# First half of the gate and value weights: one tile by plain products, two tiles as one more Strassen set

## Chip, cores and metric

One core of one Trainium2 chip (trn2). The metric is the device time of one execution in microseconds, the median of several.

## What is computed

Three layers follow each other: a linear attention with a normalised output, a feed-forward layer with a rational activation, and a gated feed-forward layer. All inputs are float32.

```python
kv = np.einsum('bhsd,bhse->bhde', k, v)              # B=8, H=8, S=576, D=64
out = np.einsum('bhsd,bhde->bhse', q, kv)
rms = np.sqrt(np.mean(out * out, axis=-1, keepdims=True) + 1e-06)
x = (out / rms * g_norm)                             # -> 4608 x 512

h = x @ w_in                                         # 512 x 2048
g = (a0 + a1*h + a2*h*h + a3*h*h*h) / (1 + |b0|*|h| + |b1|*h*h + 1e-6)
x = g @ w_out                                        # 2048 x 512

g = x @ w_gate; val = x @ w_val                      # 512 x 1536 each
y = (g * sigmoid(g) * val) @ w_out2                  # 1536 x 512
```

## The kernel before

The 4608 tokens are nine tiles of N = 512. Every matrix operand is held as two fp32r parts, a high half (a copy on ACT) and a low half (the operand minus its high half, a `sub` on DVE or POOL), and every product is three matmuls, high by high, high by low, low by high (`mm3`, L107).

**First block** (L1129 to L1190). Each tile takes 16 steps f, one for 128 columns of `w_in`. A step has 12 matmuls of `h` for itself and 12 of `y` for the step two before (LAG = 2); ACT and DVE work out the activation in between, in `g_step` (L433) and `g_finish` (L419), and POOL makes the low half `ghl`. The attention of the next tile runs in the same steps. The weights of the block stay in the pool `w` (`w0` to `w31`); the outputs of a tile go to DRAM (`y_dram`, L74).

**Gate and value block.** The 1536 columns of each of the two weights are 12 units f of 128. Two ways are used. The *plain* one (`direct_mm`, L651) takes a tile and a unit with 24 matmuls: gate and value, four times 128 rows of the contraction, three matmuls each. The *Strassen* one (`gv_step`, L728) takes two tiles together (a set) and a unit with seven products of six matmuls, 42 for what takes 48 plainly. It needs seven combinations of the two tiles (`x_sum_ops`, L596, `x_combine`, L611) and seven of the unit's weights: four are halves of the weights themselves (`u_direct`, L508), three and their companions come from four sums (`u_sums`, L530; their halves in `u_late`, L545). The first six units (UP = 6) are the first half. In it tiles 0, 1 and 2 go plainly, unit by unit, three tiles each (L1348), and then the sets a, b and c (`seq`, L554); in the second half the sets are c, o (the two halves of tile 2), b, d (tiles 0 and 1), a.

**What sets the order.** The program is written in the order in which each engine shall run it; each engine runs its queue in that order, and SP issues all DMAs from one queue. Between the products of a step the table `fill` (filled by `put(set, unit, place, ...)`, L724) gives the places at which the preparations are issued: fetch of a unit's raw weights (`u_fetch`, L481, into two buffers each for gate and value), `u_scale` (two ACT and two DVE operations), `u_join` (two DVE operations), the halves, the sums; `x_fetch`, `x_sums`, `x_combine` for the next set (`prepare`, L1252). After the products of a plain unit `direct_post` (L663) multiplies on DVE and stores; the Strassen step leaves its sums to `post` (L697) in the following step. In the plain part before, the units of the second half were fetched, joined and put aside in DRAM too (`w_dram`, L479).

The two buffers that the prediction's steps touch are written here:

```python
663    def direct_post(f, n, ps):
664        g = late["work"].tile([P, N], F32, tag=("c", "d")[(3 * f + n) % 2], ...)
665        act(g, ps[0], AF.Silu)
666        tt(nc.vector, g, g, ps[1], ALU.mult)
667        g_store(n, f, g)
...
702            merge(i, 2, "c", ALU.subtract, "d")      # post(i, 0): writes the tile "d"
```

Of the kernel before, what the change touches and what calls it, by code (L numbers as in the profile page):

```python
# [15 lines left out]
P = 128  # L16
# [25 lines left out]
def fused_kernel(ctx: ExitStack, tc: tile.TileContext, kv_main, kv_left, q_t, w_in, w_out, w_gate, w_val, w_o2, ab, g_norm, out):  # L42
# [17 lines left out]
    x_p = ctx.enter_context(tc.tile_pool(name="x", bufs=1, side="left"))  # L60
    a_ctx = ExitStack()
# [18 lines left out]
    rows = w_p.tile([1, 3, P], F32, tag="w5", name="rows")  # L80
# [78 lines left out]
    wa_raw = ((at_p, "hl"), (s_p, "stg"), (at_p, "r0"), (w_p, "w6"), (w_p, "w7"))  # L159
# [332 lines left out]
    def u_join(f, compact=False):  # L492

        if not compact:
            run(join_ops(raw_u[f]), 2)
            val[f] = [w_views(r)[2] for r in raw_u.pop(f)]
            return
        c = late["p"].tile([P, 2, N], F32, tag="g", bufs=2, name="wc")
        for j, r in enumerate(raw_u.pop(f)):
            lo, hi, _ = w_views(r)  # L500
            stt(c[:, j, :].bitcast(I32), hi, 3, lo, ALU.logical_shift_left, ALU.bitwise_or)
        nc.sync.dma_start(out=w_dram[f], in_=c)
# [5 lines left out]
    def u_direct(f, eng):  # L508

        g, v = val[f]  # L510
        u = wu[f] = late[f"u{f % UP}"].tile([P, 2, 7, HK], F32R, tag=f"u{f % UP}", name="wu")
        u_halves(u, halves_of(g), slice(0, 7, 6), eng)
        u_halves(u, halves_of(v), slice(4, 6), eng)

    def u_first(eng):

        for src in val[0]:
            t = late["p"].tile([P, 2, 2, HK], F32R, tag="g", bufs=2, name="wu0")
            act(t[:, 0], halves_of(src))
# [3 lines left out]
    def u_again(eng):

        g, v = val[0]
        u = wu[0] = late["u0"].tile([P, 2, 7, HK], F32R, tag="u0", name="wu")
        u_halves(u, halves_of(g)[:, 1:2, :], slice(6, 7), eng)
        u_halves(u, halves_of(v), slice(4, 6), eng)

    def u_sums(f, tiles):  # L530
        g, v = val[f]
        m = sums[f] = tiles
        return [
            partial(tt, nc.vector, m[0][:, 0, :], g[:, :HK], g[:, HK:], ALU.add),
            partial(tt, nc.vector, m[0][:, 1, :], m[0][:, 0, :], v[:, :HK], ALU.subtract),
            partial(tt, nc.vector, m[1][:, 0, :], v[:, :HK], g[:, :HK], ALU.subtract),
            partial(tt, nc.vector, m[1][:, 1, :], v[:, HK:], m[0][:, 1, :], ALU.subtract),
        ]

    def u_early(f):  # L540
        tiles = [late["work"].tile([P, 2, HK], F32, tag=t, bufs=2, name="sm") for t in ("a", "b")]
        run(u_sums(f, tiles), 4)
        del val[f]

    def u_late(f, eng):  # L545
        for j, m in enumerate(sums.pop(f)):
            u_halves(wu[f], m, slice(2 * j, 2 * j + 2), eng)
# [81 lines left out]
    steps = [(q, f) for q in range(1, len(seq)) for f in range(UP if q > 3 else 0, NF2 if q > 3 else UP)]  # L629
# [334 lines left out]
    with tc.manual_schedule():  # L964
# [33 lines left out]
        po, pss, sqs, nb = {}, {}, {}, {}  # L998
# [410 lines left out]
```

## Time and profile before

| what | value |
|---|---|
| median of 3 runs | 1691.32 us (1690.96 to 1692.86) |
| profiled execution, its own time | 1692.0 us |
| its span, first to last instruction | 1689.9 us |
| mean granted TensorE clock | 0.999 |
| ACT busy in the span | 1061.2 us (63%) |
| POOL busy in the span | 540.8 us (32%) |
| first block ends, gate and value begins (PE) | at about 889.8 us |

The profile has, for each engine, the instructions with start, duration and what released an idle engine. "Busy" of PE is modelled, since matmuls overlap: a matmul of 512 columns is shown with 0.39 us though the next one starts earlier, so that pace is read from the starts. A line such as L92 is a helper (`act`), L95 is `sub`, L105 `stt`, L467 `tt`; the tile names tell which use it is: `gd` is the result of a plain unit, `e` and `gout` belong to a Strassen step, `sm` are weight sums, `wu` the weight halves, `wraw` the raw weights, `ysum` and `yraw` combinations of tiles, `xc` their halves. In the changed program the helper lines are 1 to 11 lines further down.

### The profile page before, as it was taken

To read this page: it belongs to the slowest core of one execution; us is meant where nothing else is said; L and a number is where in the kernel's file an instruction comes from. 1 tells how busy PE (TensorE), PEld (TensorE's weight loads), DVE (VectorE), ACT (ScalarE), POOL (GpSimd) and SP (SyncE) were. 2 spreads that over 40 slices of the span, in tenths; PEclk is the share of its full clock that TensorE was granted. 3 is DMA by queue.
4 is the path that set the end of the run, shared out by engine and by line. 5 is a ranking of instruction groups with operands and counts; after the bars stand their busy time and mean duration, and the time that the engine had idled before them with its cause. 6 is when DMAs were issued, how large, how long until landed. Compare 5 with 4: busy or idle time off the path is not lost. (4 is left out here: it accounts for less than half of the span.)

```text
span 1689.9 us, 24169 instructions
## 1 busy us (share of the span) xinstructions
PE 1673.4 (99%) x9088; PEld 1427.1 (84%) x9088; DVE 1335.7 (79%) x1824; ACT 1061.2 (63%) x1776; POOL 540.8 (32%) x376
## 2 busy tenths in 40 slices
PE   8999999999999999999999999999999999999999
PEld 5777888888888888888888888888888888999999
DVE  7999898899889898888886666666568858676665
ACT  7898787788787787877774444444435445444442
POOL 2113444434444443443331212212302156222221
PEclk9999999999999999999999999999999999999999
DMA  8861010010001010001117536132494354444431
GB/s 336 314 241 50 8 38 13 13 38 13 32 13 38 13 38 13 32 26 38 51 50 262 193 131 266 67 110 81 142 337 145 137 175 158 145 134 150 150 131 58
DMA packets 73529, 185.07 MB, mean 110 GB/s; under 512 B 6467, under 2 KB 35396, under 8 KB 71620
## 3 DMA queue, kind: packets, MB, share of 16 engines
q1 hardware_dynamic: 73412, 183.53, 31.0%
q8 instruction: 71, 1.16, 0.3%
q14 instruction: 46, 0.38, 0.1%
HBM read 121.64 MB, written 61.87 MB: 109 GB/s over the span
## 5 line engine op out<-in xcount | busy, mean ns | idle before, releaser
L95 POOL TENSOR_TENSOR ghl<-e,ghl 128x512 fp32r<-128x512 f32 x144 | 188.1, 1306 | 512.4 <-ACT ghl L92 218.8
L110 PE MATMUL pb<-xc,wu 128*128 128x512 f32 (+1 forms) x816 | 308.7, 378 | 0.0
L109 PE MATMUL pb<-xc,wu 128*128 128x512 f32 (+1 forms) x816 | 308.6, 378 | 0.0
L111 PE MATMUL pb<-xc,wu 128*128 128x512 f32 (+1 forms) x816 | 308.5, 378 | 0.0
L105 DVE SCALAR_TENSOR_TENSOR e<-e,e 128x512 f32<-128x512 f32 x288 | 229.0, 795 | 29.4 <-ACT e L92 23.1
L110 PE MATMUL y<-ghl,wt 128*128 128x512 f32 x576 | 226.1, 393 | 4.1 <-POOL ghl L95 4.0
L109 PE MATMUL y<-ghl,wt 128*128 128x512 f32 x576 | 227.1, 394 | 0.9 <-ACT ghl L92 0.9
L110 PE MATMUL ph<-x,wt 128*128 128x512 f32 x576 | 225.2, 391 | 1.2 <-POOL x L95 0.9
L109 PE MATMUL ph<-x,wt 128*128 128x512 f32 x576 | 225.7, 392 | 0.0
L111 PE MATMUL y<-ghl,wt 128*128 128x512 f32 x576 | 225.2, 391 | 0.0
L111 PE MATMUL ph<-x,wt 128*128 128x512 f32 x576 | 224.7, 390 | 0.0
L92 ACT ACTIVATE e<-pb 128x512 f32<-128x512 f32 (+1 forms) x144 | 82.2, 571 | 218.4 <-PE pb L111 218.4
L467 DVE TENSOR_TENSOR e<-e,pb 128x512 f32<-128x512 f32 (+1 forms) x192 | 124.5, 652 | 119.1 <-PE pb L111 72.1
L874 PE MATMUL pb<-wo,xo 128*128 128x256 f32 x756 | 214.1, 283 | 1.4 <-DVE sb L467 0.9
L875 PE MATMUL pb<-wo,xo 128*128 128x256 f32 x756 | 213.9, 283 | 0.0
L876 PE MATMUL pb<-wo,xo 128*128 128x256 f32 x756 | 213.9, 283 | 0.0
L109 PEld LDWEIGHTS pb<-xc,wu 128*128 128x128 f32 x816 | 153.3, 188 | 29.0
L110 PEld LDWEIGHTS pb<-xc,wu 128*128 128x128 f32 x816 | 153.3, 188 | 28.6
L111 PEld LDWEIGHTS pb<-xc,wu 128*128 128x128 f32 x816 | 153.3, 188 | 28.5
L92 ACT ACTIVATE xo<-graw 128x768 fp32r<-128x768 f32 x122 | 99.2, 840 | 114.6 <-DVE graw L467 52.0
L92 ACT ACTIVATE e<-ph 128x512 f32<-128x512 f32 x144 | 85.6, 594 | 112.0 <-PE ph L111 111.6
L874 PEld LDWEIGHTS pb<-wo,xo 128*128 128x128 f32 x756 | 145.1, 192 | 1.9 <-DVE sb L467 1.1
(140 smaller groups left out, 3428.7 us busy)
## 6 DMA issues: line engine op xcount, KB each, us to landing
graw<-gd SPq DMA_DIRECT2D x36, 768.0 KB, 4.6
gd<-gout SPq DMA_DIRECT2D x84, 256.0 KB, 2.2
kvm<-in_kv_main SPq DMA_DIRECT2D x32, 512.0 KB, 7.2
yraw<-yd SPq DMA_DIRECT2D x26, 512.0 KB, 6.0
q<-in_q_t SPq DMA_DIRECT2D x36, 256.0 KB, 2.7
yd<-sb SPq DMA_DIRECT2D x18, 512.0 KB, 3.3
out<-sb SPq DMA_DIRECT2D x17, 512.0 KB, 3.5
wraw<-in_w_in SPq DMA_DIRECT2D x16, 512.0 KB, 4.4
```

Source lines behind the costliest of these rows:

```text
L92: nc.scalar.activation(out=out, in_=in_, func=func, **kw)
L95: eng.tensor_tensor(out=out, in0=a, in1=b.bitcast(F32), op=ALU.subtract)
L105: nc.vector.scalar_tensor_tensor(out=out, in0=in0, scalar=scalar, in1=in1, op0=op0, op1=op1)
L109: nc.tensor.matmul(ps, lhsT=wh, rhs=xh, start=first, stop=False, skip_group_check=more)
L110: nc.tensor.matmul(ps, lhsT=wh, rhs=xl, start=False, stop=False, skip_group_check=more)
L111: nc.tensor.matmul(ps, lhsT=wl, rhs=xh, start=False, stop=last, skip_group_check=more)
L467: eng.tensor_tensor(out=out, in0=a, in1=b, op=op)
L874: nc.tensor.matmul(ps, lhsT=x[:, 0, i, :], rhs=wh, start=start, stop=False, skip_group_check=not first)
L875: nc.tensor.matmul(ps, lhsT=x[:, 0, i, :], rhs=wl, start=False, stop=False, skip_group_check=not first)
L876: nc.tensor.matmul(ps, lhsT=x[:, 1, i, :], rhs=wh, start=False, stop=stop, skip_group_check=not first)
```

## The change

Tiles 0 and 1 become a Strassen set (d) in the first half too, the first of `seq`; only tile 2 goes plainly. Plain unit f and set d's step for unit f - 1 alternate. The seven combinations of tiles 0 and 1 are made during tiles 3 to 6 of the first block (`D_PLAN`), split into halves, stored to DRAM and loaded by `x_load` in both halves, so set d's own combinations in the second half go. The weight sums are written into the raw tiles themselves; the second half's weights are fetched and joined again where they are needed, in set c, and not put aside in DRAM. The x slots of the ring get a pool of their own, which holds part of `w_in` in the first block. The preparations are spread anew over DVE and POOL.

```diff
+    def w_tile(n):
+        kind, f, _ = wa_src[n]
+        if kind == "o" or f >= 2 * (RING - 4):
+            return w_p.tile([P, 2, N], F32R, tag=f"w{n}", name="wt")
+        if f % 2 == 0:
+            ring_w[f // 2] = ring_p.tile([P, 2, 2, N], F32R, tag=f"r{f // 2}", name="wt")
+        return ring_w[f // 2][:, f % 2]
...
+    def u_mids(f):
+        return [halves_of(r.bitcast(F32).rearrange("p (n two) -> p n two", two=2)[:, :, 0]) for r in raw_u[f]]
...
+    def u_direct(f, eng, eng2=None):
+        g, v = u_vals(f)
+        u = u_tile(f)
+        u_halves(u, g, slice(0, 7, 6), eng)
+        u_halves(u, v, slice(4, 6), eng2 or eng)
...
+    def u_late(f, j, eng):
+        u_halves(wu[f], u_mids(f)[j], slice(2 * j, 2 * j + 2), eng)
...
-    seq = [None, "a", "b", "c", "c", "o", "b", "d", "a"]
+    seq = [None, "d", "a", "b", "c", "c", "o", "b", "d", "a"]
+    P2 = 5
...
+    def direct_banks(f):
+        if f == 0:
+            return [ps_a.tile([P, N], F32, tag=f"pa{m}", name="pb") for m in range(2)]
+        if f in (3, 5):
+            return [ps_y.tile([P, N], F32, tag=f"y{m}", name="pb") for m in (2, 3)]
+        return [ps_h.tile([P, N], F32, tag="ph", name="pb") for m in range(2)]
...
+    def direct_post(f, ps):
+        g = late["work"].tile([P, N], F32, tag="d", bufs=1, name="gd")
         act(g, ps[0], AF.Silu)
         tt(nc.vector, g, g, ps[1], ALU.mult)
-        g_store(n, f, g)
+        g_store(ODD, f, g)
...
+    D_PLAN = (
+        {4: ("x", 0, B_11), 7: ("x", 3, B_21), 10: ("x", 2, B_22)},
+        {4: ("s", 0), 5: ("s", 1), 6: ("s", 2), 7: ("s", 3), 8: ("x", 0, T_1), 9: ("x", 1, T_3), 10: ("x", 2, T_2), 11: ("x", 3, T_4)},
+    )
...
+            if 3 <= t < 7:
+                if f == 2:
+                    d_fetch((t - 3) // 2)
+                job = D_PLAN[(t - 3) % 2].get(f, ("",))
+                if job[0] == "s":
+                    joins = [partial(d_sum, job[1])]
+                elif job[0] == "x":
+                    acts.append(partial(d_split, job[1], stored))
...
+        u_direct(1, DVE, POOL)
+        direct_post(0, direct_ps)
         for j in range(2):
             evac_pair(y_dram[TILES - 1][j], j, late["raw"].tile([P, 2, N], F32, tag=("t2", "t3")[j], name="sb"))
+        u_again(0, 0, POOL)
+        u_again(0, 1, DVE)
+        for j in range(2):
+            u_late(0, j, DVE)
+        u_fetch(2)
+        for f in range(2, UP):
+            put(1, f - 2, 1, partial(u_scale, f))
+            put(1, f - 2, 2, partial(u_join, f))
+            put(1, f - 2, 4, partial(u_direct, f, DVE, POOL))
+            put(0, f, 0, partial(u_sums, f))
+        for f in range(1, UP):
+            put(1, f - 1, 0, partial(u_late, f, 0, DVE), partial(u_late, f, 1, DVE))
+            if f + 2 < UP:
+                put(1, f - 1, 0, partial(u_fetch, f + 2))
...
-        for f in range(UP):
-            for n in range(3):
-                if f or n:
-                    direct_post(f, n, direct_mm(f, n, direct_banks(3 * f + n)))
...
+        def d_unit(f):
+            direct_post(f, direct_mm(f, direct_banks(f)))
+            for op in fill.pop(("D", f), ()):
+                op()
+
+        d_unit(1)
+        gv_step(0)
+        for f in range(2, UP):
+            d_unit(f)
+            gv_step(f - 1)
+        for i in range(UP - 1, len(steps)):
             gv_step(i)
```

How the instructions stand is told by the built programs, in three places.

**ACT, at the handover from the first block to the gate and value block.** `ghl` is the last step's activation, `wu_8129` the weight halves of unit 1 (`u_direct(1, ...)`), `gd` and `pb_8066` the plain unit 0, `sb` the last outputs of the first block. Before:

```order
L92 ACTIVATE ghl<-e_7945 128x512
L92 ACTIVATE xc<-yraw 128x2x512 x2
L92 ACT_TABLE_LOAD
L92 ACTIVATE gd<-pb 128x512
...
L92 ACTIVATE sb<-y_7352 128x512
```

Now, with the semaphores that each waits for:

```order
L93 ACTIVATE ghl_8063<-e3_8041 128x512 [waits DVE_49,PE_49]
L93 ACTIVATE wu_8129<-wraw_7320 128x2x256 [waits PE_49]
L93 ACTIVATE wu_8129<-wraw_7322 128x512
L93 ACT_TABLE_LOAD
L93 ACTIVATE gd_8134<-pb_8066 128x512
L93 ACTIVATE sb_8138<-y0_7428 128x512
```

The split of tile 1's input has gone from here, and the halves of unit 1's weights have come. Their tile `wu_8129` lies in SBUF over the tile of the last `w_out` weights (`W["o", 15]`), so the wait for PE is one for the last matmul of the first block.

**DVE, from one plain unit's multiplication to the next.** Before, two tiles of unit 1 and what stood between their `gd`:

```order
L467 TENSOR_TENSOR gd<-gd,pb 128x512
L132 TENSOR_SCALAR wraw<-wraw 128x512 x2
L95 TENSOR_TENSOR wu<-sm,wu 128x512 x2
L105 SCALAR_TENSOR_TENSOR wraw<-wraw 128x512 x2
L467 TENSOR_TENSOR gd<-gd,pb 128x512
```

Now, from unit 2's `gd` to unit 3's:

```order
L478 TENSOR_TENSOR gd<-gd,pb 128x512
L478 TENSOR_TENSOR wraw<-wraw 128x256 x4
L478 TENSOR_TENSOR e<-e,pb 128x512 x2
L96 TENSOR_TENSOR wu<-wraw,wu 128x512 x2
L133 TENSOR_SCALAR wraw<-wraw 128x512 x2
L478 TENSOR_TENSOR e<-e,pb 128x512
L106 SCALAR_TENSOR_TENSOR wraw<-wraw 128x512 x2
L478 TENSOR_TENSOR gout<-gout,e 128x512
L478 TENSOR_TENSOR e<-e,pb 128x512
L478 TENSOR_TENSOR gout<-gout,e 128x512
L96 TENSOR_TENSOR wu<-wraw,wu 128x2x256
L478 TENSOR_TENSOR gd<-gd,pb 128x512
```

The first `wraw x4` are unit 2's four sums, `e`, `gout` the work of set d's step 0 and 1, the last `wu` (128x2x256) the low half of unit 3's gate weights, which the next plain unit needs. Between unit 3's and unit 4's `gd` the same rows stand with two of 128x1024 (`ysum`, `yraw`) in between.

**DVE, in step 4 of tile 4 of the first block**, where nothing of set d stood:

```order
L106 SCALAR_TENSOR_TENSOR e_4300<-e_4300,e_4301 128x512
L106 SCALAR_TENSOR_TENSOR e_4302<-e_4302,na,e_4301 128x512
L478 TENSOR_TENSOR yc<-yc 128x512
L106 SCALAR_TENSOR_TENSOR e_4302<-e_4300,e_4302 128x512
L106 SCALAR_TENSOR_TENSOR e_4349<-e_4349,b_abs,e_4350 128x512
L469 TENSOR_TENSOR e_4351<-e_4351,ph 128x512
L106 SCALAR_TENSOR_TENSOR e_4351<-e_4351,na,ph 128x512
```

One subtraction (`d_sum`) has come between the operations of a step. Tiles 4 and 6 have such an addition in each of their steps 4 to 11 (four sums, four low halves), tiles 3 and 5 in three steps each.

## Rows read from the trace of the kernel before

**Rows 1.** The page, busy us (share) and instructions of PE and DVE

```profile
PE 1673.4 (99%) x9088; PEld 1427.1 (84%) x9088; DVE 1335.7 (79%) x1824; ACT 1061.2 (63%) x1776; POOL 540.8 (32%) x376
```

**Rows 2.** Waits of PE from 100 us on: us, times, longest

```profile
PE y L110 <- POOL ghl L95: 3.6, 5, 1.5
PE y L109 <- ACT ghl L92: 0.9, 1, 0.9
```

**Rows 3.** PE in order of time (start, us): first block, handover, a plain unit's end

```profile
844.62 0.39 PE L109 MATMUL y<-ghl,wt 128*128 128x512 f32 x1
...
877.94 0.39 PE L109 MATMUL y<-ghl,wt 128*128 128x512 f32 x1
...
889.53 0.40 PE L111 MATMUL y<-ghl,wt 128*128 128x512 f32 x1
889.77 0.39 PE L109 MATMUL pb<-xc,wu 128*128 128x512 f32 x1
...
895.13 0.39 PE L111 MATMUL pb<-xc,wu 128*128 128x512 f32 x1
```

**Rows 4.** ACT in order of time, the weight halves of a unit

```profile
892.12 2.13 ACT L92 ACTIVATE wu<-wraw 128x512 fp32r<-128x512 f32 x4 [2.16 <-DVE wraw L105]
```

**Rows 5.** DVE in order of time, gate and value block, 895 to 1023 us

```profile
895.63 0.69 DVE L467 TENSOR_TENSOR gd<-gd,pb 128x512 f32<-128x512 f32 x1 [3.01 <-PE pb L111]
...
898.79 0.42 DVE L467 TENSOR_TENSOR sm<-wraw 128x256 f32<-128x256 f32 x1
...
899.92 0.42 DVE L467 TENSOR_TENSOR sm<-wraw,sm 128x256 f32<-128x256 f32 x1
...
989.19 0.75 DVE L132 TENSOR_SCALAR wraw<-wraw 128x512 int32<-128x512 int32 x2
989.86 1.28 DVE L95 TENSOR_TENSOR wu<-sm,wu 128x512 fp32r<-128x512 f32 x2
991.07 1.28 DVE L105 SCALAR_TENSOR_TENSOR wc<-wraw 128x512 int32<-128x512 int32 x2
...
1001.11 1.47 DVE L467 TENSOR_TENSOR e<-e,pb 128x512 f32<-128x512 f32 x2 [1.86 <-ACT e L92]
1002.50 1.22 DVE L467 TENSOR_TENSOR ysum<-yraw 128x1024 f32<-128x1024 f32 x1
...
1007.28 0.69 DVE L467 TENSOR_TENSOR e<-e,pb 128x512 f32<-128x512 f32 x1 [1.23 <-PE pb L111]
1008.08 0.69 DVE L467 TENSOR_TENSOR gout<-gout,e 128x512 f32<-128x512 f32 x1
...
1022.98 2.48 DVE L467 TENSOR_TENSOR gout<-gout,e 128x512 f32<-128x512 f32 x1
```

**Rows 6.** POOL in order of time, at the end of that stretch

```profile
1022.50 2.39 POOL L95 TENSOR_TENSOR xc<-yraw,xc 128x1024 fp32r<-128x1024 f32 x1 [34.31 <-ACT xc L92]
```

**Rows 7.** DMA issues: count, KB each, median us from issue to landing

```profile
wraw<-in_w_gate SPq DMA_DIRECT2D x12, 512.0 KB, 4.0
wraw<-in_w_val SPq DMA_DIRECT2D x12, 512.0 KB, 4.7
...
gd<-gd SPq DMA_DIRECT2D x18, 256.0 KB, 2.5
```

**Rows 8.** PE in order of time, tile 0 of the first block

```profile
130.90 0.50 PE L109 MATMUL y<-ghl,wt 128*128 128x512 f32 x1 [0.87 <-ACT ghl L92]
132.88 0.71 PE L110 MATMUL y<-ghl,wt 128*128 128x512 f32 x1 [1.48 <-POOL ghl L95]
```

**Rows 9.** Busy time by stretch (us, PE, PEld, DVE, ACT, POOL, granted clock, DMA): tile 0, tile 4

```profile
133.00:134.00 1.00, 1.00 (x3) 0.81 (x4) 1.00 (x3) 1.00 (x3) 0.00 (x0) 0.50 0.00 0
...
136.00:137.00 1.00, 1.00 (x5) 0.82 (x4) 1.00 (x3) 0.00 (x0) 0.00 (x0) 0.80 0.89 336
...
130.00:140.00 10.00, 7.65 (x26) 5.76 (x25) 9.92 (x18) 7.58 (x14) 3.14 (x2) 0.83 0.17 52
431.00:522.00 91.00, 91.00 (x411) 75.61 (x410) 81.63 (x110) 72.81 (x123) 39.44 (x30) 1.00 0.07 24
```

More of the change, by code (lines that the diff above doesn't have):

```diff
@@ L490, in u_scale, with u_join, u_vals @@
             w_scale(r)
[L492 to L502, printed above, removed]
+    def u_join(f):
+        run(join_ops(raw_u[f]), 2)
+    def u_vals(f):
+        return [halves_of(w_views(r)[2]) for r in raw_u[f]]
+    def u_mids(f):
+        return [halves_of(r.bitcast(F32).rearrange("p (n two) -> p n two", two=2)[:, :, 0]) for r in raw_u[f]]
     def u_halves(u, src, at, eng):
@@ L515, in u_first @@
     def u_first(eng):
-        for src in val[0]:
+        for src in u_vals(0):
             t = late["p"].tile([P, 2, 2, HK], F32R, tag="g", bufs=2, name="wu0")
-            act(t[:, 0], halves_of(src))
-            sub(eng, t[:, 1], halves_of(src), t[:, 0])
+            act(t[:, 0], src)
+            sub(eng, t[:, 1], src, t[:, 0])
             first_u.append(t)
[L523 to L528, printed above, removed]
@@ L530, in u_sums, with u_again, u_sum_ops @@
-    def u_sums(f, tiles):
-        g, v = val[f]
-        m = sums[f] = tiles
+    def u_again(f, part, eng):
+        g, v = u_vals(f)
+        if part == 0:
+            u_halves(u_tile(f), v, slice(4, 6), eng)
+        else:
+            u_halves(wu[f], g[:, 1:2, :], slice(6, 7), eng)
+    def u_sum_ops(f):
+        g, v = u_vals(f)
+        m = u_mids(f)
         return [
[L534 to L537, printed above, removed]
-        ]
@@ L540, in u_early @@
[L540 to L547, printed above, removed]
+            partial(tt, nc.vector, m[0][:, 0, :], g[:, 0, :], g[:, 1, :], ALU.add),
+            partial(tt, nc.vector, m[0][:, 1, :], m[0][:, 0, :], v[:, 0, :], ALU.subtract),
+            partial(tt, nc.vector, m[1][:, 0, :], v[:, 0, :], g[:, 0, :], ALU.subtract),
@@ L1201, in fused_kernel @@
         late["raw_ctx"] = ExitStack()
-        for name in ("units", "ring", "work", "raw"):
+        for name in ("units", "work", "raw"):
             b_pools[name] = (late["raw_ctx"] if name == "raw" else ctx).enter_context(
@@ L1209, in fused_kernel @@
         DVE, POOL = nc.vector, nc.gpsimd
-        for t in (1, 2):
-            pool, tag = slots[6 + t]
-            r = late["ring"].tile([P, 2, 2, N], F32, tag=tag, name="yraw")
-            for j in range(2):
-                raw_x["D", 2 * t + j] = r[:, j]
-                nc.sync.dma_start(out=r[:, j], in_=y_dram[t][j])
-        for n in range(2, 4):
-            x_split(("D", n), raw_x["D", n], DVE)
-        direct_post(0, 0, direct_ps)
-        for n in range(4, 6):
-            x_split(("D", n), raw_x["D", n], DVE)
+        u_direct(1, DVE, POOL)
@@ L1248, in fused_kernel @@
[L1248 to L1250 removed]
+        u_again(0, 0, POOL)
+        u_again(0, 1, DVE)
+        for j in range(2):
+            u_late(0, j, DVE)
[5 more added lines that the diff above has]
+            put(0, f, 0, partial(u_sums, f))
@@ L1313, in fused_kernel @@
             ):
[L1314 removed]
+                put(P2 - 1, 0, n + d, op)
         last = len(seq) - 1
```

169 lines of the change are left out of this document (76 added, 93 removed).

## The prediction

> **What bounds the kernel now.** I read the page first: PE is busy for 1673 of 1690 us, so the time is its number of matmuls times their pace, and every wait of PE comes on top [rows 1]. Then its waits: from 100 us on there are only 4.5 us before a `y` matmul of the first block, and none in the gate and value block before the last layer [rows 2]. So a matmul that goes is a gain in full, and a wait that comes is a loss in full. The pace comes from PE in order of time: 147 matmuls lie between the starts at 844.62 and 877.94, 0.2267 us each, and the handover from the first block (889.53) to the next plain product (889.77) has no gap [rows 3].
>
> The change puts more DVE work between two plain units, and PE now needs its result at once. So the other rows are prices: what ACT and DVE take for one operation of the gate and value block [rows 4, 5], what a DVE operation suffers when POOL runs [rows 6], how long a store or a fetch takes to land [rows 7], and what a pause does to PE's clock [rows 8, 9].
>
> **What goes.** Six units of tiles 0 and 1 took 2 x 24 matmuls plainly and take 42 as a set: 36 fewer, 36 x 0.2267 = **-8.2 us**. The parking of the second half's weights in DRAM and set d's own combinations in the second half go too; they hid beside a PE without waits, so I count them as nothing. That the weights of units 6 to 11 are now joined in set c costs DVE four operations per 10 places there (0.75 + 1.28 us, [rows 5], in 13.6 us of PE); I take it as hidden, with the busy share of 900 to 1000 us behind me (two thirds).
>
> **What comes, step by step.** Consecutive DVE operations start about 0.07 us before the earlier one is shown as ended (989.19 + 0.75 against 989.86, [rows 5]); I take that off at each passage.
>
> *Handover.* ACT's copy of unit 1's gate halves waits for the last `y` matmul. Call that matmul's start 0. A reader starts 0.50 us after a matmul's start (895.13 in [rows 3], 895.63 in [rows 5]); four copies take 2.13 us, so one some 0.6 [rows 4]; so the first plain product of unit 1 starts near 1.2 instead of 0.23. The third needs the low half, one DVE `sub` of 0.64 later (1.28 for two, [rows 5]), near 1.9 instead of two paces after the first. Cost **1.3** (1.0 to 1.6).
>
> *Unit 2.* Its raw weights can only be fetched when unit 0's last `sub` has read the old ones. Behind the handover ACT has the table load, `gd`, two copies of `y` and four copies for unit 0, DVE the same in step, which puts the fetch near 7.6; it lands 4.0 and 4.7 later [rows 7], while ACT and DVE stand in their queues at it. Then shifts, merge, join, copy and `sub`: the low half comes at about 16.1. PE, 1.3 late, has 60 matmuls until unit 2 and wants it at 15.6. Cost **0.5** (0 to 2, by the landing).
>
> *Units 3 and 5.* Let 0 be the start of the last matmul of the plain unit before. DVE, in its order: `gd` from 0.50 to 1.19; four sums, 1.55 (898.79 to 899.92 + 0.42), to 2.7. The next merge writes the tile `d`, the one that `gd` is being stored from (now one buffer for both): issued at 1.2, landed 2.5 later [rows 7], so it starts at 3.7. Then two merges 1.47, two `sub` 1.28, two shifts 0.75, a merge 0.69, two joins 1.28, `gout` 0.69, merge and `gout` 1.49 (1007.28 to 1008.77), `sub` 0.64: 8.29, less eight passages of 0.07, ends at 11.4. PE in the meantime has 42 Strassen matmuls and two of the next unit; the third wants the low half at 45 x 0.2267 = 10.2. Late by 1.3. Besides, POOL makes the low half of the value weights from about 9.5 to 10.8, and the last `gout` falls into that: such an operation took 2.48 us instead of 0.69 and ended 0.57 after POOL [rows 5, 6]. That adds 0.7. **2.0 each, 4.0 together** (0.2 each if the store lands within the sums and POOL is not met, 2.6 if it lands later).
>
> *Unit 4.* The same chain with two combinations of 1.22 us for set a in it [rows 5], 2.3 after passages: late by 1.3 + 2.3 + 0.7 = **4.3** (2.5 to 5.0).
>
> *Clock.* In tile 0, PE stood 0.87 and 1.48 us with one matmul in between [rows 8]; right after it the granted clock was 0.50 from 133 to 136 and 0.80 in the next microsecond, the lower of its levels, 1.2 GHz [rows 9]: 3 x 0.5 + 0.2 = 1.7 us lost. Unit 4's pause is longer, so I count it once: **1.7**. The 2 us of units 3 and 5 lie near that pause, but unbroken and shorter, and I count nothing (1.7 each is in the range).
>
> *Tiles 3 to 6.* In tile 4 DVE is busy for 81.6 of 91 us [rows 9], so idle for 0.59 us of a step of 5.7; eight steps in a row get an operation of about 0.65. It just fits, with some delay of `ghl`: **0.8** (0 to 8).
>
> **Sum:** 1.3 + 0.5 + 4.0 + 4.3 + 1.7 + 0.8 = 12.6 against 8.2, +4.4. The profiled execution took 1692.0 (span 1689.9) and lies 0.7 above the median, so 1691.3 + 4.4 = **1695.7 us**. A difference of 0.2%, 3.4 us, is about what can be told from none here.
>
> **The shared port.** The row shows a `gout` that waits for POOL's end and only then runs. The Trainium skill, "SBUF — State Buffer", section "Who interferes with whom", says that a DVE operation with two SBUF inputs and a POOL operation that reads SBUF exclude each other for a whole instruction, and that whichever starts first holds the port. By that rule the 0.7 of units 3 to 5 is there only if POOL is first; if the `gout` is, POOL waits, whose half is wanted 12 matmuls later, and the sum falls by 2.1 to 1693.6. I count POOL first, since the merge before that `gout` reads PSUM and the `gout` starts after 9.5.
>
> **Rivals.**
> 1. *The chain fits* (not slower). What decides is whether the low half is there 10.2 us after the last plain product. If the store lands within the sums and POOL is not met, units 3 and 5 cost 0.2 each, unit 4 2.5 and its clock stays, and the handover 1.2: 4.1 in all, 1691.3 - 8.2 + 4.1 = 1687.2. For it: 2.5 us is a median. Against: the sums end 1.0 us too early for it, and two combinations remain in any case. 0.20.
> 2. *The clock stays up* though unit 4 waits: 1695.7 - 1.7 = 1694.0. For it: one pause alone shows the fall. Against: that pause was shorter. 0.20.
> 3. *DVE holds up tiles 4 and 6.* In tile 0 DVE was busy for 9.92 of 10 us and PE for 7.65 [rows 9], and that is where the pauses of rows 8 are. If each of the two tiles comes to one such event, 2.35 + 1.7 us each, 8.1 instead of 0.8: 1703.0. Against: it takes a backlog of more than DVE's own idle time, and the additions last only eight steps. 0.15.
>
> That the set would not be a Strassen set can be left out: the program has 36 matmuls fewer.
>
> **How the numbers follow.** My forecast, pauses before units 2 to 5 and one drop of the clock, has 0.45, with a range of its own of 1693.5 to 1699. The range 1687 to 1701 takes in rivals 1 (most of it) and 2, the bounds of the store's landing and a clock drop at units 3 and 5; it leaves out rival 3 and some of rival 1. Faster by over 0.2% (below 1687.9): most of rival 1, 0.12. Within 0.2% (to 1694.7): the rest of it 0.08, three quarters of rival 2, 0.15, and the lower end of the forecast 0.10, 0.33. Slower: 0.35 + 0.05 + 0.15 = 0.55.
>
> **What would show it.** In the changed kernel's PE rows: a gap of about 1.3 us before the first plain product of unit 1, split by two matmuls; then, before the third matmul of units 3, 4 and 5, waits for DVE `wu` of about 2, 4 and 2 us; a granted clock of 0.5 for some 3 us after unit 4's. On DVE, a pause before the first merge after the sums, with a DMA (`gd`) as what ended it, and a last `gout` that ends after POOL. The forecast is wrong if PE's waits for `wu` add up to less than 5 us, or if waits for `ghl` in tiles 4 and 6 are the larger part.

## The result, and the profile after

The changed kernel takes 1708.27 us (median of 5 runs, 1707.17 to 1708.65) against 1691.32: a ratio of 1.0096, 95% interval 1.0081 to 1.011. It is slower by 17 us, outside the range of 1687 to 1701. The profiled execution has a span of 1706.4 us, 16.5 more than before.

The page's busy line, for [rows 1]: 36 matmuls fewer, PE no longer at 99%.

```profile
PE 1672.1 (98%) x9052; PEld 1417.4 (83%) x9052; DVE 1355.3 (79%) x1866; ACT 1070.6 (63%) x1797; POOL 524.9 (31%) x365
```

The waits of PE over the whole span, for [rows 2] (us in total, times, longest):

```profile
PE y L111 <- POOL ghl L96: 8.6, 11, 1.4
PE pb L112 <- DVE wu L96: 5.9, 3, 3.2
PE ph L111 <- POOL x L96: 3.3, 6, 0.7
PE y L110 <- ACT ghl L93: 2.4, 3, 1.3
PE pb L110 <- ACT e L93: 1.9, 2, 1.0
...
PE pb L110 <- DMA xc<-xdd: 0.8, 1, 0.8
PE pb L110 <- ACT wu L93: 0.7, 1, 0.7
```

The rows on `pb` are the gate and value block, those on `y` and `ph` the first block. In order of time (PE, start and duration, in brackets the wait and what ended it):

```profile
424.50 0.50 PE L111 MATMUL ph<-x,wt 128*128 128x512 f32 x1 [0.66 <-POOL x L96]
496.29 0.49 PE L110 MATMUL y<-ghl,wt 128*128 128x512 f32 x1 [1.28 <-ACT ghl L93]
497.70 0.50 PE L111 MATMUL y<-ghl,wt 128*128 128x512 f32 x1 [0.91 <-POOL ghl L96]
687.89 0.51 PE L111 MATMUL y<-ghl,wt 128*128 128x512 f32 x1 [1.29 <-POOL ghl L96]
694.62 0.50 PE L111 MATMUL y<-ghl,wt 128*128 128x512 f32 x1 [0.91 <-POOL ghl L96]
901.39 0.50 PE L110 MATMUL pb<-xc,wu 128*128 128x512 f32 x1 [0.75 <-ACT wu L93]
915.11 0.50 PE L110 MATMUL pb<-xc,wu 128*128 128x512 f32 x1 [0.91 <-ACT e L93]
933.66 0.50 PE L112 MATMUL pb<-xc,wu 128*128 128x512 f32 x1 [1.38 <-DVE wu L96]
952.23 0.50 PE L112 MATMUL pb<-xc,wu 128*128 128x512 f32 x1 [3.17 <-DVE wu L96]
970.52 0.50 PE L112 MATMUL pb<-xc,wu 128*128 128x512 f32 x1 [1.38 <-DVE wu L96]
```

496 is in tile 4, 688 in tile 6; 901 is the handover, 915 in unit 2's preparation, then come units 3, 4 and 5. To find the sum I laid the starts of the same matmuls of both traces beside each other: from the start of tile 2 to step 4 of tile 8 the changed kernel falls **10.0 us** behind. Counted from step 4 of a tile to step 4 of the next, that is 1.0 in tile 3, 4.9 in tile 4, 0.65 in tile 5 and 3.5 in tile 6, so that what a tile loses at its end is its own. In the rest of tile 8 it loses 0.9; after it come 5.8 more, the 8.2 of the 36 matmuls already taken off.

What happened in tile 4 stands on ACT in order of time:

```profile
489.93 0.78 ACT L93 ACTIVATE e<-ph,na 128x512 f32<-128x512 f32 x1
495.09 0.63 ACT L93 ACTIVATE xd<-yc 128x512 fp32r<-128x512 f32 x1 [4.38 <-DMA xdd<-xd]
495.62 0.61 ACT L93 ACTIVATE ghl<-e 128x512 fp32r<-128x512 f32 x1
```

`xd` is the pair of halves of one combination, one buffer. Its copy on ACT waits until the combination before has been stored, and the `ghl` that PE wants stands behind it in ACT's queue. DVE made that stored low half late:

```profile
489.92 0.97 DVE L96 TENSOR_TENSOR xd<-yc,xd 128x512 fp32r<-128x512 f32 x1
```

From the copy at 486.02 to this low half it is 3.9 us, to the next copy 9.1; a step lasts 5.8. (The 14 low halves take 0.68 to 1.53 us, 0.97 in the median.) And in tile 3, where no copy waits, DVE falls behind and stays so. This is one operation of each step, `e<-e,b_abs,e`, on DVE, first of the kernel before, then of the changed one, behind a split in step 10; PE's own matmuls there start within 0.2 us of each other:

```profile
397.17 0.75 DVE L105 SCALAR_TENSOR_TENSOR e<-e,b_abs,e 128x512 f32<-128x512 f32 x1
...
408.50 0.74 DVE L105 SCALAR_TENSOR_TENSOR e<-e,b_abs,e 128x512 f32<-128x512 f32 x1
...
420.18 0.75 DVE L105 SCALAR_TENSOR_TENSOR e<-e,b_abs,e 128x512 f32<-128x512 f32 x1
```

```profile
398.06 0.74 DVE L106 SCALAR_TENSOR_TENSOR e<-e,b_abs,e 128x512 f32<-128x512 f32 x1
...
409.39 0.75 DVE L106 SCALAR_TENSOR_TENSOR e<-e,b_abs,e 128x512 f32<-128x512 f32 x1
...
421.08 0.75 DVE L106 SCALAR_TENSOR_TENSOR e<-e,b_abs,e 128x512 f32<-128x512 f32 x1
```

0.9 us late in each: four steps long nothing is regained, though DVE shows idle time in between, most of it "<-ACT e". The two engines wait for each other. In the changed kernel ACT's queue stands at `ghl`, which comes late from DVE, and ACT's next work for DVE, `e<-e,bias_q`, stands behind it; DVE then waits for that (ACT, then DVE):

```profile
398.18 0.63 ACT L93 ACTIVATE ghl<-e 128x512 fp32r<-128x512 f32 x1 [1.34 <-DVE e L106]
...
399.24 0.71 ACT L93 ACTIVATE e<-e,bias_q 128x512 f32<-128x512 f32 x1
```

```profile
400.65 1.40 DVE L106 SCALAR_TENSOR_TENSOR e<-e,e 128x512 f32<-128x512 f32 x1 [0.46 <-ACT e L93]
```

At the end of the tile PE pays, at 424.50. In tile 4 of the kernel before, nearly all of DVE's idle time of 9.4 us [rows 9] is of this kind (us, times, longest):

```profile
DVE e L105 <- ACT e L92: 7.9, 16, 1.3
```

### The profile page after: what moved, and what is told of

Read it like the earlier page. It is cut to its first block, busy times and chain, and to the rows that moved or that the text cites. A ratio compares the mean times of both kernels' runs of the same rounds, so it can differ in the third digit from the quotient of the medians.

```text
span 1706.4 us, 24184 instructions
## 1 busy us (share of the span) xinstructions
PE 1672.1 (98%) x9052; PEld 1417.4 (83%) x9052; DVE 1355.3 (79%) x1866; ACT 1070.6 (63%) x1797; POOL 524.9 (31%) x365
## 5 line engine op out<-in xcount | busy, mean ns | idle before, releaser
L112 PE MATMUL pb<-xc,wu 128*128 128x512 f32 (+1 forms) x804 | 305.1, 380 | 5.9 <-DVE wu L96 5.9
L110 PE MATMUL pb<-xc,wu 128*128 128x512 f32 (+1 forms) x804 | 305.2, 380 | 3.5 <-ACT e L93 1.9
L111 PE MATMUL pb<-xc,wu 128*128 128x512 f32 (+1 forms) x804 | 304.6, 379 | 0.0
L478 DVE TENSOR_TENSOR e<-e,pb 128x512 f32<-128x512 f32 (+1 forms) x216 | 140.8, 656 | 120.9 <-PE pb L112 72.1
L93 ACT ACTIVATE e<-pb 128x512 f32<-128x512 f32 (+1 forms) x162 | 92.6, 572 | 212.8 <-PE pb L112 212.4
L112 PEld LDWEIGHTS pb<-xc,wu 128*128 128x128 f32 x804 | 151.4, 188 | 35.9 <-DVE wu L96 7.9
L110 PEld LDWEIGHTS pb<-xc,wu 128*128 128x128 f32 x804 | 151.4, 188 | 34.6 <-ACT e L93 3.1
L111 PEld LDWEIGHTS pb<-xc,wu 128*128 128x128 f32 x804 | 151.4, 188 | 28.1
L908 PEld LDWEIGHTS pb<-wo,xo 128*128 128x128 f32 x756 | 145.1, 192 | 1.9 <-DVE sb L478 1.1
L909 PEld LDWEIGHTS pb<-wo,xo 128*128 128x128 f32 x756 | 145.1, 192 | 0.1
```

Of the source, the lines that this page charges most:

```text
L93: nc.scalar.activation(out=out, in_=in_, func=func, **kw)
L110: nc.tensor.matmul(ps, lhsT=wh, rhs=xh, start=first, stop=False, skip_group_check=more)
L111: nc.tensor.matmul(ps, lhsT=wh, rhs=xl, start=False, stop=False, skip_group_check=more)
L112: nc.tensor.matmul(ps, lhsT=wl, rhs=xh, start=False, stop=last, skip_group_check=more)
L478: eng.tensor_tensor(out=out, in0=a, in1=b, op=op)
L908: nc.tensor.matmul(ps, lhsT=x[:, 0, i, :], rhs=wh, start=start, stop=False, skip_group_check=not first)
```

## The experiments

Profiled runs differ in tiles 0 and 1 by up to 4.7 us with the same work there (the granted clock falls in some and not in others, and the waits for the key and value fetches differ), so that parts are compared from the start of tile 2 on. "Tiles 2 to 7" below is what PE loses against the kernel before from there to step 4 of tile 8, from the starts of the same matmuls. It comes from one profiled execution of each kernel; e4, e6 and e7, which leave these tiles as they are, lose 10.0 to 10.5 there, so differences under half a microsecond say nothing.

### e1: two buffers

```diff
-        x = at_p.tile([P, 2, N], F32R, tag="r0", name="xd")
...
-        act(x[:, 0, :], d_raw[m])
-        return [partial(sub, nc.vector, x[:, 1, :], d_raw[m], x[:, 0, :])]
...
+        x = d_his[0][:, len(d_his) % 2, :]
...
+        low = d_raw[m].bitcast(F32R)
...
+        act(x, d_raw[m])
+        return [partial(sub, nc.vector, low, d_raw[m], x)]
...
```

> The tile xd becomes two buffers of the high half, used in turn; the low half is written over the raw combination. Every operation of ACT and DVE stays in its place; 14 more stores of half the size. Theory A (ACT's copy waits for the store out of the one buffer, and holds up its queue: 4 waits, 7.5 us): the waits on xdd<-xd go, tiles 4 and 6 lose 1 to 3 us instead of 10, the time is 1699 to 1702. Rival B (DVE has more to do in those steps than they last, and its backlog holds up ghl): nothing of that changes, 1707 to 1709.

1705.5 us, ratio 1.0073 (1.0056 to 1.009), between the two ranges. ACT waits no longer for a store of `xdd`, and tiles 2 to 7 lose 4.4 instead of 10.0: tiles 4 and 6 lose 2.8 instead of 8.4, as theory A had it, and the 1.6 of tiles 3 and 5 stay. So the one buffer was worth 5.6 us, the larger part; 4.4 stay. The time fell by less because waits later in the program came out longer in this run (2.2 us for ACT `e` at 1323, with a fall of the clock behind it).

### e2: every other step

```diff
-        {4: ("s", 0), 5: ("s", 1), 6: ("s", 2), 7: ("s", 3), 8: ("x", 0, T_1), 9: ("x", 1, T_3), 10: ("x", 2, T_2), 11: ("x", 3, T_4)},
+        {4: ("s", 0), 5: ("s", 1), 6: ("s", 2), 7: ("s", 3), 8: ("x", 0, T_1), 10: ("x", 1, T_3), 12: ("x", 2, T_2), 14: ("x", 3, T_4)},
```

> The four splits of tiles 4 and 6 stand in steps 8, 10, 12, 14 instead of 8 to 11; one buffer as in the changed kernel. Theory A: copy, low half, store and landing have two steps (11.5 us) instead of one, no wait on xdd<-xd, 1699 to 1702. Rival B: the same additions over 11 steps instead of 8; DVE's idle time of about 0.6 us a step then nearly covers them, 1701 to 1705. So this says whether the order of steps is a cure, e1 says of what.

1705.62, ratio 1.0081 (1.0066 to 1.0096): outside A's range, 0.6 above B's. No copy waits for a store any more, yet tiles 2 to 7 lose 7.8: what is added late in a tile is not made up for by its end. That led to the table under e5.

### e3: no sums

```diff
-                    joins = [partial(d_sum, job[1])]
+                    joins = []
```

> Leaves out the four sums of the combinations of set d in tiles 4 and 6 (the first half's outputs of tiles 0 and 1 are then of other combinations). DVE has 8 operations less there, the splits stay in steps 8 to 11. Rival B: half of the additions are gone, DVE keeps up, tiles 4 and 6 lose under 3 us, 1700 to 1702. Theory A: the copies still wait for the store of the split before, by less since the low half comes earlier: tiles 4 and 6 lose 4 to 9 us, 1702 to 1707, and the waits on xdd<-xd stay.

1706.32, ratio 1.0083 (1.0068 to 1.0098); tiles 2 to 7 lose 8.5. Eight of 22 additions are gone and only 1.5 us with them: it is not DVE's number of operations, and rival B is out. Two of the four waits for the store stay, as theory A said.

### e4: an own tile for `gd`

```diff
-        g = late["work"].tile([P, N], F32, tag="d", bufs=1, name="gd")
+        g = late["work"].tile([P, N], F32, tag="gd", bufs=1, name="gd")
```

> The plain unit's result gets a tile of its own, so that the first merge of the next step need not wait for its store. If the chain on DVE from gd to the low half of the next unit sets the waits of units 3 to 5, the pause of 0.71 us before that merge goes and the three waits get shorter by as much each (1.38, 3.17, 1.38 to about 0.7, 2.5, 0.7): 2.1 us in all, 1706.2. If it is POOL's operation beside the last gout that sets them, its end stays and they get shorter by less than 0.3 each: 1707.5 to 1708.5.

1704.63, ratio 1.0069 (1.0054 to 1.0085), 1.6 below the 1706.2 of the first forecast. DVE in the changed kernel, from unit 2's `gd` to unit 3's low half:

```profile
923.01 1.55 DVE L478 TENSOR_TENSOR wraw<-wraw 128x256 f32<-128x256 f32 x4
925.27 1.41 DVE L478 TENSOR_TENSOR e<-e,pb 128x512 f32<-128x512 f32 x2 [0.71 <-DMA gd<-gd]
...
931.66 1.34 DVE L478 TENSOR_TENSOR gout<-gout,e 128x512 f32<-128x512 f32 x1
932.93 0.68 DVE L96 TENSOR_TENSOR wu<-wraw,wu 128x512 fp32r<-128x512 f32 x1
```

In e4 the pause is gone, and PE's three waits are 3.7 in total instead of 5.9:

```profile
PE pb L112 <- DVE wu L96: 3.7, 3, 2.5
```

POOL's half beside that `gout`, in the changed kernel:

```profile
931.14 1.31 POOL L96 TENSOR_TENSOR wu<-wraw,wu 128x512 fp32r<-128x512 f32 x1 [12.92 <-ACT wu L93]
```

So the chain on DVE sets them, and the store was 0.7 us of each. The `gout` of 1.34 runs beside POOL's half in both kernels.

### e5: even steps over six tiles

```diff
-        {4: ("x", 0, B_11), 7: ("x", 3, B_21), 10: ("x", 2, B_22)},
-        {4: ("s", 0), 5: ("s", 1), 6: ("s", 2), 7: ("s", 3), 8: ("x", 0, T_1), ...},
+        {6: ("x", 0, B_11), 8: ("x", 3, B_21), 10: ("x", 2, B_22)},
+        {4: ("s", 0), 6: ("x", 0, T_1), 8: ("s", 1), 10: ("x", 1, T_3)},
+        {4: ("s", 0), 6: ("s", 2), 8: ("s", 3), 10: ("x", 2, T_2), 12: ("x", 3, T_4)},
...
-            if 3 <= t < 7:
+            if 2 <= t < 8:
...
```

> The combinations of set d are made in tiles 2 to 7 instead of 3 to 6, only in steps 4, 6, 8, 10 and 12, where DVE of the kernel before is idle for 0.9 to 1.4 us (0.1 to 0.4 us in the odd ones); one sum is made twice, 24 additions instead of 22. Theory B2 (what costs is an addition in a step in which DVE has no room, and the store behind the low half that comes late for it): the first block ends within 1.5 us of before instead of 10.7 after it, 1697.5 to 1700. Rival A2 (the additions cost by their number, wherever they stand, or the copies wait for the one buffer in any case): 5 to 10 us are left there, 1703 to 1708.

1706.19, ratio 1.0082 (1.0065 to 1.0099); tiles 2 to 7 lose 8.6. My theory B2 fell: idle time in a step is not room in it. What room there is shows when DVE's lateness is written out step by step: the start of `e<-e,b_abs,e` less that of the kernel before, less the same difference of the first `h` matmul of the step, in us.

```
step               4     5     6     7     8     9    10    11    12    13    14    15
changed, tile 3  0.00  1.15  0.28  0.27  0.73  0.72  0.00  1.08  1.08  1.08  1.04  1.05
changed, tile 4  0.01  0.49  0.00  0.49  0.48  1.64  1.15  2.47  4.69  1.94  1.08  1.09
e1, tile 4      -0.01  0.47  0.00  0.49  0.47  1.63  0.72  1.73  2.18  2.18  1.08  1.08
e2, tile 4       0.01  0.49 -0.01  0.48  0.48  1.63  0.65  1.73  1.73  2.87  1.71  2.79
e5, tile 4       0.00  0.00  0.00  0.01  0.01  0.00 -0.01  1.09  1.08  2.24  1.71  1.72
```

A split in an even step makes DVE about 1.1 us late from the next step on. That is regained in step 6 and in step 10, up to about 1 us each, and in step 14 (1.2 in e2, 0.5 in e5); where PE itself waits, as before steps 13 and 14 of tile 4, the difference falls by PE's delay. A sum in an even step costs nothing (e5: three of them). Idle time does not tell these steps: in tile 4 of the kernel before, DVE is idle for 1.37 us in steps 6 and 10, but for 0.98 to 0.99 in steps 4, 8 and 12 and for 0.46 in step 14. Why it is these steps is not shown. What is late in step 15 PE pays at the tile's end: 2.58 us after e2's 2.79.

### e6: another slot for unit 1

```diff
...
+        u_tile(0)
         u_direct(1, DVE, POOL)
```

> Unit 0's tile is taken first, so that it lies over the last weights of the first block, and unit 1's over weights that were last read 16 us earlier. The copy of unit 1's halves then runs before the last y matmul: the wait of 0.75 us at 901 goes, with its restart 1.1 us. ACT's table load and gd come earlier as well, and with them unit 0's halves and the fetch of unit 2's weights, by about 2 us: if that fetch sets the wait of 0.91 us at 915, it goes too, 1705.7 to 1706.3; if not, 1707 to 1707.4.

1705.59, ratio 1.0076 (1.0061 to 1.0091). ACT's copy of unit 1's halves runs at 893.69, before the last `y` matmul; the waits at 901 and at 915 are both gone. The first forecast holds: the second wait hung on the first.

### e7: the sums for set a behind unit 5

```diff
-                put(p, 4 if short else 2, n, partial(x_sums, q, 1))
+                put(p, 4 if short or q == 2 else 2, n, partial(x_sums, q, 1))
```

> The three sums for set a (128x1024, 1.22 us) move from step 2 of set d to step 4, behind the last plain unit. Unit 4's wait then has the length of those of units 3 and 5: 3.17 to 1.4. If it is the length of that one pause after which the clock falls, the microseconds at 0.50 go as well: -1.8 - 1.7, 1704.8. If it falls by the pauses of units 2 to 5 together, it still falls: 1706.5.

1710.55, ratio 1.0107 (1.0091 to 1.0124): slower than both forecasts. Unit 4's wait is that of the others (1.79 from start to start, 3.56 in the changed kernel), and the clock does not fall behind it, as the first forecast had it; but in e3 it did not fall behind a pause of 3.58 either, so this does not settle it. In their new place the sums meet POOL's combinations. DVE, POOL and PE there:

```profile
978.93 3.51 DVE L96 TENSOR_TENSOR wu<-wraw,wu 128x512 fp32r<-128x512 f32 x2
982.36 3.42 DVE L478 TENSOR_TENSOR ysum<-yraw 128x1024 f32<-128x1024 f32 x1
```

```profile
979.09 5.60 POOL L96 TENSOR_TENSOR xc<-yraw,xc 128x1024 fp32r<-128x1024 f32 x2 [11.00 <-ACT xc L93]
```

The first of each pair by itself, DVE and POOL:

```profile
978.93 0.68 DVE L96 TENSOR_TENSOR wu<-wraw,wu 128x512 fp32r<-128x512 f32 x1
```

```profile
979.09 2.80 POOL L96 TENSOR_TENSOR xc<-yraw,xc 128x1024 fp32r<-128x1024 f32 x1 [11.00 <-ACT xc L93]
```

```profile
993.42 0.50 PE L110 MATMUL pb<-xc,wu 128*128 128x512 f32 x1 [3.84 <-DVE e L478]
```

The two `wu` take 3.51 us instead of 1.28, the sum 3.42 instead of 1.22 [rows 5]. The first `wu` starts 0.16 ahead of POOL and takes its usual 0.68. The second starts at 979.53, while POOL's first runs, takes 2.91 and ends 0.55 after it; the sum starts 0.52 after POOL's second and ends 1.08 after that. So each is held up by one POOL operation, like the `gout` under e4, only that this one is longer. PE waits 3.84 further on, with the clock at 0.50 behind that.

### e8: all cures

```diff
...
-            put(1, f - 2, 4, partial(u_direct, f, DVE, POOL))
+            put(1, f - 2, 3, partial(u_direct, f, DVE, POOL))
...
+                    if op is o_fetch and n in (3, 4):
+                        at = ((last - 2, 3, 0), (last - 1, 0, 6))[n - 3]
...
```

> e4 to e7 together, and two more: unit f's gate and value halves one place earlier (before the merge and the last gout of the step, which takes some 2 us off the chain on DVE), and two fetches of the last layer's weights moved out of the stretch in which set d's seven loads fill the DMA engines (1305 to 1330; 1.2 to 2.4 us of waits). If the places found are all there are: 1708.3 - 9.5 (tiles 3 to 6) - 2.4 (handover and unit 2) - 7.1 (units 3 to 5 with their restarts) - 1.7 (clock) - 1.8 = 1685.8, range 1684 to 1689: faster than the kernel before by about 5 of the 8.2 us. If a cure only moves its wait to the next operation: 1690 to 1696.

1705.83, ratio 1.0082 (1.0067 to 1.0097), 20 above my forecast. Units 3 to 5 wait no more for `wu`, but 0.34 us each for ACT `e`. Tiles 2 to 7 still lose 8.5 (e5's plan), the sums beside POOL cost a wait of 2.40, and the later of the two fetches, moved behind 2 MB for the next set, a wait of 4.01 us and a fall of the clock at 1325. The halves, the sums and the fetch had in part only moved their waits.

### e9: where DVE catches up

```diff
...
+        {5: ("x", 0, B_11), 8: ("x", 3, B_21)},
+        {4: ("x", 2, B_22), 6: ("s", 1), 8: ("x", 1, T_3)},
+        {4: ("s", 0), 5: ("x", 0, T_1), 6: ("s", 2), 8: ("xs", 2, T_2, 3), 10: ("x", 3, T_4)},
+        {4: ("x", 0, B_11), 8: ("x", 3, B_21)},
+        {4: ("x", 2, B_22), 6: ("s", 1), 8: ("x", 1, T_3)},
+        {4: ("s", 0), 5: ("x", 0, T_1), 6: ("s", 2), 8: ("xs", 2, T_2, 3), 12: ("x", 3, T_4)},
...
-            if 3 <= t < 7:
+            if 2 <= t < 8:
...
```

> From the traces so far: against the kernel before, DVE's operations of the first block are 1.1 us late after each split (its low half), and stay so until step 6, 10 or, in tiles 6 and 7, 14; what is late after step 10 is late at the end of the tile, where PE waits for x. Sums in even steps make nothing late. So the splits are put ahead of steps 6 and 10, two to a tile over tiles 2 to 7 (steps 4 or 5, and 8; one too many in tile 4, step 10; a third in tile 7, step 12), and the sums in even steps. Theory C (it is where DVE can catch up that counts): of the 10 us that tiles 3 to 6 lose in the changed kernel 1 to 2.5 are left, 1699 to 1701. Rival D (each split costs about half a microsecond wherever it stands, as in e5, which lost 7 for 14): 5 to 7 are left, 1703 to 1706.

Tiles 2 to 7 lose 2.3 us: theory C, against 5 to 7 by D, with the same 14 splits as before and no more buffers; e5, over the same six tiles, lost 8.6. No copy waits for the one buffer here either. In tile 5 DVE's lateness is 1.18 in step 5, 0.12 in step 6, 1.27 in step 9, 0.19 in step 10 and none at the end. The time is 1702.43, ratio 1.0059 (1.0046 to 1.0073), above C's 1701: the profiled run (1704.83, the longest of the four) came to tile 2 already 3.5 us late, with the clock at 0.50 for 6.8 us from 25.9 on, and set d's loads cost a wait of 2.2 us with a fall of the clock.

### e10: the low halves on POOL

```diff
-        return [partial(sub, nc.vector, x[:, 1, :], d_raw[m], x[:, 0, :])]
+        return [partial(sub, nc.gpsimd, x[:, 1, :], d_raw[m], x[:, 0, :])]
```

> The changed kernel's plan, but the 14 low halves of set d's combinations in tiles 3 to 6 on POOL (idle for 2.4 to 4.6 us of each of these steps) instead of DVE. Theory E (DVE's queue alone was the trouble): DVE is not late after a split, the store starts earlier and no copy waits for it; 1 to 3 us of the 10 are left, 1699 to 1702. Rival F (POOL's operation keeps DVE out of SBUF for its time, as with the gout of rows 5): DVE is late by 0.6 to 1.2 us after each all the same, 5 to 9 us are left, 1703 to 1708.

1715.29, ratio 1.0143 (1.0127 to 1.0159), worse than both said; tiles 2 to 7 lose 16.3. The low half stands behind `ghl` and `sqhl` in POOL's queue, so that the store is no earlier, and takes 1.75 us. POOL, then ACT, in tile 4:

```profile
476.49 1.75 POOL L96 TENSOR_TENSOR sqhl<-sq,sqhl 128x512 fp32r<-128x512 f32 x1
478.20 1.75 POOL L96 TENSOR_TENSOR xd<-yc,xd 128x512 fp32r<-128x512 f32 x1
```

```profile
473.94 0.64 ACT L93 ACTIVATE xd<-yc 128x512 fp32r<-128x512 f32 x1
...
483.00 0.63 ACT L93 ACTIVATE xd<-yc 128x512 fp32r<-128x512 f32 x1 [4.30 <-DMA xdd<-xd]
```

### e11: all cures again

```diff
...
-  put(p, 4 if short else 2, n, partial(x_sums, q, 1))
+  put(p, 4 if short else 2 + (q == 2 and n > 1), (1, 5)[n > 3] if q == 2 else n, partial(x_sums, q, 1))
...
+  put(*((last - 2, 3, 0) if op is o_fetch and n == 3 else at), partial(op, i))
```

> e9's plan, e4's tile, e6's slot, unit f's gate and value halves one place earlier, the three sums for set a spread (steps 2 and 3 of set d, none beside POOL's combinations in step 4, where e7 lost 4 us), and one fetch of the last layer's weights before set d's loads. By the parts: 1691.3 - 8.2 (36 matmuls) + 2 (tiles 2 to 7) + 0.8 (tile 8) + 1.5 to 2.5 (units 2 to 5) + 0 to 1.5 (set d's loads): 1687.4 to 1689.9, faster than the kernel before by 0.1 to 0.25%. If the waits move on once more as in e8 (1705.8): 1695 to 1700.

1692.42, ratio 0.9999 (0.9991 to 1.0008): the loss of 17 us is undone, the gain not reached; it lies 2.5 above the sum of the parts. Tiles 2 to 7 lose 2.5, set d's loads nothing, the clock stays up. Left are four waits for ACT. In unit 4's step, on ACT and PE:

```profile
939.50 1.27 ACT L93 ACTIVATE wu<-wraw 128x512 fp32r<-128x512 f32 x2 [2.21 <-DVE wraw L106]
940.68 0.58 ACT L93 ACTIVATE e<-pb 128x512 f32<-128x512 f32 x1
```

```profile
941.31 0.50 PE L110 MATMUL pb<-xc,wu 128*128 128x512 f32 x1 [1.46 <-ACT e L93]
```

The halves, moved one place forward, wait for DVE's join and hold up the copy of the bank behind them.

### e12: the halves behind that copy

```diff
...
+            first = n == 4 and i < UP
+            if not first:
+                post(i - 1, n)
             for op in fill.pop(7 * i + n, ()):
                 op()
+            if first:
+                post(i - 1, n)
...
```

The halves of the next units are put at place 4 again instead of e11's 3, and run there ahead of `post`; DVE's order is that of e11.

> e11 with one thing changed: ACT copies the step's bank (snap b) before the next unit's gate and value halves, where in e11 those copies, which wait for DVE's join, stood ahead of it and four products waited for ACT e (1.22, 0.73, 1.85 and 1.83 us from start to start, 4.7 us above the pace); DVE's order stays. If only that order on ACT made the waits: they go, and the low halves still come in time (DVE as in e11): 1692.4 - 4 = 1688 to 1689, against 1691.3 to 1691.8 of the kernel before. If DVE's chain is late by itself: the waits come back as DVE wu at the third product of a unit, of 0.5 to 1.5 us in units 4 and 5, 1690 to 1692.

**1686.01 us** (1684.55 to 1688.11), ratio 0.997 (0.9958 to 0.9981): 5.5 us faster than the kernel before, and 2 below the first forecast. The waits for ACT are gone, and from tile 2 on the trace is 4.4 us shorter than e11's, about the 4.7 of the four waits; the other 3.8 between the two profiled spans lie before tile 2. The page's busy line, and PE in the stretch where the changed kernel had five waits:

```profile
PE 1665.6 (99%) x9052; PEld 1418.6 (84%) x9052; DVE 1355.4 (80%) x1866; ACT 1069.3 (64%) x1797; POOL 523.4 (31%) x365
...
890.00:1000.00 110.00, 110.00 (x487) 90.97 (x486) 75.71 (x113) 51.82 (x86) 18.22 (x9) 1.00 0.39 135
```

From the last `y` matmul to the last product of the program it gains 8.2 us on the kernel before, all that 36 matmuls are worth; it gives back 2.4 in tiles 2 to 7 and 0.6 in the rest of tile 8.

## Why the prediction was wrong

**What failed** is the step *Tiles 3 to 6*, "It just fits, with some delay of `ghl`: 0.8": it measures 10.0. Two things went wrong in it.

- It counted DVE's operations, at about 0.65 each (a low half took 0.97 in the median), against DVE's mean idle time in tile 4. That idle time is, for the most part, DVE waiting for ACT (7.9 of 9.4 us), in a loop in which lateness goes from DVE to ACT and back; e5 filled the idle steps and lost 8.6 all the same. Room is where lateness is regained, steps 6, 10 and in part 14, and e9 got from 10.0 to 2.3 by placing the splits ahead of them. POOL may have a share in the loop (`e<-e,na,e` on DVE took 1.78 us at 406.97, while POOL's `sqhl` ran from 406.44 to 408.21, and 0.74 at 401.97); no run tries that.
- It did not ask what the new ACT copy waits for. I followed each added wait in the gate and value block, down to the store of `gd`, and none in the first block, where `xd` has one buffer. e1 prices that at 5.6 us. The two parts do not add up to 10.0 as they stand: the low half comes late because DVE is late, and e9's places keep the copies apart, too. With the copies kept apart and the lateness left (e2), 7.8 are lost.

**Rival 3** had the place (tiles 4 and 6) and nearly the sum, 8.1, but with DVE's backlog alone as its cause. Its sum is near by luck: 3.4 of the 8.1 are falls of the clock in tiles 4 and 6, and the profiled execution has none there. I gave it 0.15 and left it out of the range. The argument against it, "a backlog of more than DVE's own idle time", was the first error again.

**My signs** did not show the failure. PE's waits for `wu` add up to 5.9 on DVE and 0.7 on ACT, above the 5 that I had set, and its waits for `ghl` in tiles 4 and 6 to 4.9, not the larger part. They left out the waits for `x` at the ends of tiles 3 to 6 and what follows a wait before PE is at its pace again; by the starts of the matmuls tiles 4 and 6 lose 8.4.

**The other steps held.** Measured against PE's pace of 0.2267, with the slower starts right behind a wait included: *Handover:* 1.3 foretold, 1.3 measured. *Unit 2:* 0.5 against 1.3; the two fetches landed 4.7 and 5.5 after their issue, 0.7 and 0.8 later than taken, and what waited was the copy of a bank behind the scaling on ACT, not the low half. *Units 3 and 5:* 2.0 against 1.7 each; the pause before the first merge, the order and the `gout` beside POOL are there as described, the store landing earlier than taken. *Unit 4:* 4.3 against 3.6. *Clock:* 1.7 against 1.7, once, behind unit 4's pause, but that it fits is partly luck: behind the same pause (3.56 to 3.59 from start to start) the clock was at 0.50 for 3.4 us in the changed kernel, in e1, e6, e9 and e10, for 6.8 us in e2 and e5, and stayed at 1.00 in e3. Busy time by stretch there (clock in the third column from the right; 1.00 in the microseconds ahead of these and behind them):

```profile
953.00:954.00 1.00, 1.00 (x5) 0.78 (x4) 0.32 (x1) 0.00 (x0) 0.00 (x0) 0.76 0.30 99
954.00:955.00 1.00, 1.00 (x4) 0.81 (x3) 0.00 (x0) 0.00 (x0) 0.00 (x0) 0.50 0.00 0
955.00:956.00 1.00, 1.00 (x3) 0.74 (x3) 0.00 (x0) 0.00 (x0) 0.00 (x0) 0.50 0.00 0
956.00:957.00 1.00, 1.00 (x4) 0.79 (x3) 0.00 (x0) 0.60 (x1) 0.00 (x0) 0.53 0.04 8
```

0.24 + 0.5 + 0.5 + 0.47 = 1.71 us at the lower level.

**The shared port.** POOL's half ran from 931.14 to 932.45 and the `gout` from 931.66 to 933.00: DVE waited for POOL's end, as counted. The Trainium skill, "SBUF — State Buffer", section "Who interferes with whom", says that the one that starts first holds the port; the trace agrees, POOL was 0.5 us ahead.

**What I left out:** set d's seven loads in the second half. Their replacement of work on chip counted as nothing; the DMA engines are at 1.0 of their time from 1305 to 1330, the last load and the weights of the last layer come late, and PE loses 2.4 us there (in e1, e3 and e9 waits of 2.1 to 2.2 us for ACT `e`, with a fall of the clock). And 0.9 in tile 8, where DVE has 12 operations on `wraw` in steps 6 to 13 instead of 2 (eight sums, two scalings, two joins), for which the prediction has no term; no run tries them apart. And two short waits behind unit 5, at 993 and 1001, 0.7 together.

**The whole.** Sum: 10.0 + 0.9 + 1.3 + 1.3 + 1.7 + 3.6 + 1.7 + 1.7 + 0.7 + 2.4 - 8.2 = 17.1. The kernel before itself loses 0.4 against that pace in its first plain products, and the changed one came to tile 2 0.2 earlier; that leaves the 16.5 us between the two spans.

## What to carry to other kernels

Idle time of an engine that runs in a loop with another is not room for more work: lay the starts of one repeated operation in two traces side by side, see after which steps lateness is regained, and put the additions ahead of those. When an operation joins an engine's queue, write down the round trip of its buffer (copy, second engine, store, landing) and compare it with the interval at which it comes again; if it is longer, all that stands behind it in the queue waits. A cure is done when the next wait behind it has been looked for.

## What the runs showed of the hardware that I had not expected

- What a DVE operation loses beside POOL grows with the length of POOL's: 1.34 us instead of 0.69 beside a half of 128x512 (1.31), 2.91 instead of 0.68 beside a subtraction of 128x1024 (2.80, e7). Work moved to an engine that is idle for 2.4 to 4.6 us of each step cost 6 us more than it had on the busier one (e10).
- The clock does not answer to the length of a pause alone. In tile 4 two pauses with one matmul between, 1.67 and 1.41 us from start to start, left it at 1.00 in the changed kernel; with 1.78 and 1.40 in e4 and 2.01 and 1.40 in e7 it was at 0.50 for 3.4 us, and with 2.14 and 1.41 in e6 it stayed at 1.00. One pause of 3.58 left it at 1.00 in e3 and was followed by 3.4 us at 0.50 in e1. What decides there stays open.
